# A planned attention and feed-forward kernel: other transfer costs in its planner, and an earlier second pair of heads

## The chip, the cores and the metric

The kernel runs on one core of one Trainium2 chip. The time is that of the device for one execution, in microseconds (us). The engines are TensorE (PE in the profile; PEld is its weight load), VectorE (DVE), ScalarE (ACT), GpSimd (POOL) and SyncE (SP), which issues every transfer here.

## The reference

```python
def _attn_ref(q, k, v, cap):                 # 4 batches, 12 heads, 448 positions, 64 columns
    scores = np.matmul(q, k.transpose(0, 1, 3, 2)) / np.sqrt(q.shape[-1])
    scores = cap * np.tanh(scores / cap)
    attn = np.exp(scores - np.max(scores, axis=-1, keepdims=True))
    return np.matmul(attn / (np.sum(attn, axis=-1, keepdims=True) + 1e-09), v)
def _moe_ref(x, w_in, w_out):                # 1792 x 768, 768 x 2048, 2048 x 768
    h = x @ w_in
    return (h * np.cos(h)) @ w_out
def _moe2_ref(x, w1, w2, w3, w_out):         # 768 x 1024 twice, 1024 x 1024, 1024 x 768
    return (((x @ w1) * (x @ w2)) @ w3) @ w_out
```

The output of the attention, with the heads side by side, goes through the first of the two feed-forward parts, and that through the second. The arrays of the attention are float32. The weights of the two feed-forward parts are float64.

## The kernel before

**Precision.** TensorE works on operands split into a high part (a rounded copy) and a low part (the rest). A product is then three matmuls, high by high, high by low and low by high: `mm3`, lines 389 to 391. The split is a copy (`copy`, line 363, executed at L365, L366 or L369) and a subtraction (`lo`, which goes through `tt`, L375). Weights arrive as words of 64 bits. `convert` makes float32 of them in four steps (L913 or L914, L919, L926, L930).

**Stages.** Three stages overlap in time. `columns` is the attention: the 48 heads are taken in 24 pairs, each with four chunks of 112 columns of keys, numbered g through all pairs. For a chunk, `c_S` makes the scores of two heads in a double bank of the PSUM (there are two), `c_exp` lets ScalarE take the tanh and then the exponential of them, and `c_PV` multiplies by V (L694) and sums the exponentials with a matmul by ones (L699). `c_sums` gathers the sums in four small transfers into `rs`, takes the reciprocal, writes it to `rs_d` and reads it back spread over the partitions into `rb`; `c_norm` multiplies by it on VectorE or GpSimd. `make_w34` multiplies the last two weights (w3 and w_out of the second feed-forward part) into one, in 16 runs, beside the attention. `moe1` and `moe2` are the two feed-forward parts.

**Two forms of the scores.** For the first `SLIM` pairs, `c_load` fetches q and k of a pair once (two heads on 128 partitions), `c_split` splits them, and `c_S` makes the scores with matmuls of 64 rows, two heads at once (L650). For the other pairs, `a_load` fetches each head twice, once for each half of the partitions, `a_split` puts high and low parts of k above each other, and the scores take matmuls of 128 rows (L660, L661). The tiles of q and k (`qr`, `kr`) have two planes of 448 columns and a ring of one slot. The slim form uses the first plane.

**The order of the work.** No order is written out by hand. Every operation is entered in a plan with a due time, the engines that can do it with a cost for each, what it reads and writes, and, for a transfer, its size `kb`. `schedule` simulates: at each moment it gives an idle engine the ready operation of the earliest due time, if its ring has a free slot. A due time is a rank and not a start: an operation may start before it. The order so found is fixed, and on the chip each engine takes its instructions in that order and waits for semaphores. A transfer costs 0.66 us on SyncE, then shares one line:

```python
if o.kb:
    line = max(line, end) + o.kb / self.RATE
    out = line + self.LATENCY
```

Readers of it become ready at `out` (and `HOP` later). Due times of the attention are `at(g)` = 10 + 3.03 g (lines 526 to 528); those of the first weight run lie 20 us ahead of its matmuls at 20, its loads another 14 us ahead, so -14 for the first w3 tile, and -9.1 and -6.5 for the first two w_out tiles. A load of q and k is due six chunks ahead of its pair, a split three, V two; only the first pair's q and k have -99.

**Edge.** `general` is a second program for large values of `cap` and does not run here.

Of the kernel before, what the change touches and what calls it, by code (L numbers as in the profile page):

```python
# [20 lines left out]
B, H, S, D = 4, 12, 448, 64  # L21
# [16 lines left out]
PAD = 64  # L38
# [98 lines left out]

class Plan:
    HOP = 0.25
    RATE, LATENCY = 250.0, 2.2  # L140
    SWITCH = 1.3


# [159 lines left out]
    ql=6, qs=3,  # L303
# [18 lines left out]
def tile_kernel(tc, *args):  # L322


    nc = tc.nc
    cap = args[3]
    program(tc, *args)
    with tc.tile_pool(name="large", bufs=1) as p:
        c = p.tile([1, 2], F32, name="cap2")
        large = p.tile([1, 1], mybir.dt.int32, name="large")  # L330
        nc.sync.dma_start(c[:, 0:1], cap.rearrange("(o n) -> o n", o=1))
        nc.vector.tensor_scalar(c[:, 1:2], c[:, 0:1], -1.0, None, op0=ALU.mult)
        nc.vector.tensor_tensor(c[:, 0:1], c[:, 0:1], c[:, 1:2], op=ALU.max)
        nc.vector.tensor_scalar(large, c[:, 0:1], CAP_MAX, None, op0=ALU.is_gt)
        with tc.If(nc.values_load(large[0:1, 0:1], min_val=0, max_val=1) > 0):
            program(tc, *args, general=True)
# [3 lines left out]
def program(  # L340
# [22 lines left out]
    def copy(due, dst, src, n, on, psum=False):  # L363
        opts = {
            "A": ("ACT", (0.051 if psum else 0.094) + n / 1200, lambda: ACT.copy(dst(), src())),  # L365
            "D": ("DVE", 0.068 + n / (960 if psum else 1920), lambda: DVE.tensor_copy(dst(), src()))  # L366
            + (() if psum else (True,)),
            "P": ("POOL", 0.16 + n / 1200,
                  lambda: POOL.tensor_scalar(dst(), src(), 1.0, 0.0, op0=ALU.mult, op1=ALU.add)),  # L369
        }  # L370
        plan.op(due, [opts[e] for e in on], r=[src], w=[dst])

    def tt(due, dst, a, b, n, op, on="D", psum=False):
        opts = {
            "D": ("DVE", 0.068 + n / 960, lambda: DVE.tensor_tensor(dst(), a(), b(), op=op))  # L375
            + (() if psum else (True,)),
            "P": ("POOL", 0.158 + n / 480, lambda: POOL.tensor_tensor(dst(), a(), b(), op=op)),
        }
        plan.op(due, [opts[e] for e in on], r=[a, b], w=[dst])

    def lo(due, dst, src, hi, n, on="PD", psum=False):
        tt(due, dst, src, hi.view(lambda t: t.bitcast(F32)), n, ALU.subtract, on, psum)

    def dma(due, dst, src, r=(), w=(), kb=115, write=False):
        plan.op(due, [("SP", 0.66, lambda: SP.dma_start(dst(), src()))], r=r, w=w,  # L385
                kb=kb)
# [17 lines left out]
    for name, kw in dict(const={}, xring={}, dram=dict(space=DRAM), psum=dict(space=PSUM), doubles=dict(space=PSUM), singles=dict(space=PSUM), attn={}, lp={},  # L404
                         wi=dict(side="right"), wp=dict(side="right"), yp=right, hp=right, mp=right, cv=right,
                         q2=right).items():
# [21 lines left out]
    class Scratch:  # L428
# [7 lines left out]
        def at(self, sub, pick=None):  # L436
            return Ref(self.item, sub, pick)
# [70 lines left out]
    A = {}  # L508
# [21 lines left out]
    qk, vt, st, sm, rs, rb, s_t, t_t, pt_t, ph_t, pv_t, zs_t, x32 = ({} for _ in range(13))  # L530

    def rows(j):
        return lambda t: t[j * D:(j + 1) * D]
# [4 lines left out]
    def a_load(i, g):  # L538
        b, h = divmod(i, H)
        qk[i] = A["qr"].new(), A["kr"].new()  # L540
        for it, src in zip(qk[i], (q2, k2)):
            for j in range(2):
                r = it.at(j, rows(j))
                dma(at(g) if i else -99.0, r, lambda src=src: src[b, h // 2].rearrange("(i d) s -> d i s", i=2),
                    w=[r], kb=230)
# [6 lines left out]
    def a_split(i, g):  # L552
        q, k = (Ref(x) for x in qk.pop(i))
        qh, ql, ks = (A[x].ref() for x in ("qh", "ql", "ks"))
        copy(at(g), ks, k, 2 * S, "PAD")
        low = Ref(ks.item, None, rows(1))
        lo(at(g), low, k.view(rows(1)), low, 2 * S)
        copy(at(g), qh, q, 2 * S, "PAD")
        lo(at(g), ql, q, qh, 2 * S)
        for j in range(2):  # L560
            st[i + j] = qh[:, j], ql[:, j], ks[:, j]
# [39 lines left out]


    NT = NC // 2
    SLIM = 3

    def c_load(i, g):
        if i // 2 >= SLIM:
            return a_load(i, g)
        b, h = divmod(i, H)
        qk[i] = A["qr"].new(), A["kr"].new()  # L610
        for it, src in zip(qk[i], (q2, k2)):
            r = it.at(0, lambda t: t[:, 0])
            dma(at(g) if i else -99.0, r, lambda src=src: src[b, h // 2], w=[r], kb=230)

    def c_split(i, g):
        if i // 2 >= SLIM:
            return a_split(i, g)
        q, k = (x.at(0, lambda t: t[:, 0]) for x in qk.pop(i))
        qh, ql, ks = (A[x].new() for x in ("qh", "ql", "ks"))
        kh, kl = (ks.at(j, lambda t, j=j: t[:, j]) for j in range(2))  # L620
        qh, ql = (x.at(0, lambda t: t[:, 0]) for x in (qh, ql))
        copy(at(g), kh, k, S, "PAD")
        lo(at(g), kl, k, kh, S)
        copy(at(g), qh, q, S, "PAD")
        lo(at(g), ql, q, qh, S)
        st[i] = (kh, qh), (kh, ql), (kl, qh)

    def c_consts():
# [4 lines left out]
    def cv_load(i, g):  # L633
        b, h = divmod(i, H)
        n, j = divmod(i, 2)
        if j == 0:
            vt[n] = A["v"].new()
        r = vt[n].at(j, lambda t: t[:, j])
        dma(at(g), r, lambda: v[b, h], w=[r])

    def c_S(n, k, g):
        s = s_t[n, k] = s_r.ref()
        if n < SLIM:
            terms = st[2 * n]
# [20 lines left out]
    def c_exp(n, k, g):  # L665
        s = s_t.pop((n, k))[:CP, :, :S]
        p = A["p"].ref()
        for j in range(2):
            if n < SLIM:
                ph_t[n, j, k] = p, j  # L670
# [37 lines left out]
    def c_sums(n, g):  # L708

        t, z = A["rs"].new(), zs_t.pop(n)  # L710
        for j in range(2):
            for k in range(2):
                q = Q * (2 * j + k)
                y = t.at((j, k), lambda x, j=j, k=k: x[j * D:(j + 1) * D, k])
                dma(at(g), y, z.view(lambda x, q=q: x[q:q + 1]), r=[z], w=[y], kb=100)
        r, d = Ref(t), rs_d.at(n, lambda d: d[n].rearrange("j (p c) -> (j p) c", p=D))
        s0, s1 = (r[:, k] for k in range(2))

        def f():
            DVE.tensor_tensor(s0(), s0(), s1(), op=ALU.add)  # L720
            DVE.reciprocal(s0(), s0())

        plan.op(at(g) + 3, [("DVE", 0.2, f)], r=[r], w=[r])
        dma(at(g) + 4, d, s0, r=[r], w=[d], kb=100, write=True)
        rb[n] = A["rb"].new()
        for k in range(2):
            y = rb[n].at(k, rows(k))
            dma(at(g) + 5, y, lambda k=k: rs_d.item.tile()[n, k].unsqueeze(0).to_broadcast([D, S]), r=[d], w=[y])
# [10 lines left out]
    def columns():  # L739
        one = c_consts()  # L740
        c_load(0, -2)
        c_split(0, -1)
        for g in range(-8, NT * NH + 16):
            of_pair(c_load, -G["ql"], g, NT)
            of_head(cv_load, -2, g, NT)
            of_pair(c_split, -G["qs"], g, NT)
            if 0 <= g < NT * NH:
                c_S(*divmod(g, NC), g)
                c_exp(*divmod(g, NC), g)
            of_two(lambda n, g: n < 2 and c_PV(n, [0], one, g), 3, g)  # L750
            of_two(lambda n, g: c_PV(n, [1] if n < 2 else [0, 1], one, g), 5, g)
            of_two(c_move, 6, g)
            of_two(c_sums, 6, g)
            of_two(lambda n, g: c_norm(n, at(g) + 11), 6, g)
            of_two(lambda n, g: a_out(2 * n + 1, at(g) + 14), 6, g)
        first = plan.move(s_r, hy_r, at(g), lambda k: ())
        plan.move(s_r, hy_r, at(g), lambda k: range(4), part_doubles, [first])
# [648 lines left out]
```

## Time and profile before

| | us |
|---|---|
| runs | 1070.08, 1067.01, 1069.99 (median 1069.99) |
| profiled execution, its own time | 1065.92 |
| its span, first to last instruction | 1064.1 |
| TensorE busy in it | 1045.1 (98%) |
| VectorE busy | 874.0 (82%) |
| ScalarE busy | 492.1 (46%) |
| GpSimd busy | 173.6 (16%) |

The profile is of one execution. Times in it count from its first instruction. A busy TensorE is one that has a matmul under way, and need not be at its peak rate. An idle engine costs time only where the engine that sets the end waits for it.

### The profile page before, as it was taken

To read this page: it belongs to the slowest core of one execution; us is meant where nothing else is said; L and a number is where in the kernel's file an instruction comes from. 1 tells how busy PE (TensorE), PEld (TensorE's weight loads), DVE (VectorE), ACT (ScalarE), POOL (GpSimd) and SP (SyncE) were. 2 spreads that over 40 slices of the span, in tenths; PEclk is the share of its full clock that TensorE was granted. 3 is DMA by queue.
4 is the path that set the end of the run, shared out by engine and by line. 5 is a ranking of instruction groups with operands and counts; after the bars stand their busy time and mean duration, and the time that the engine had idled before them with its cause. 6 is when DMAs were issued, how large, how long until landed. Compare 5 with 4: busy or idle time off the path is not lost.

```text
span 1064.1 us, 15654 instructions
## 1 busy us (share of the span) xinstructions
PE 1045.1 (98%) x5832; PEld 894.5 (84%) x5832; DVE 874.0 (82%) x1343; ACT 492.1 (46%) x649; POOL 173.6 (16%) x159
## 2 busy tenths in 40 slices
PE   6999998999999999999999999999999999999997
PEld 3677775777888888889999999999999999999997
DVE  7998667899999898788889878779899889667643
ACT  5877675886667665621253211122344245311121
POOL 4222110221342131210002100011313000000000
PEclk9999999999999999999999999999999999999999
DMA  7876976777667655428632422106555546221232
GB/s 232 220 215 179 245 213 188 213 202 243 203 194 235 207 159 156 154 77 277 208 104 81 144 60 59 46 15 204 189 182 193 156 136 217 98 88 60 61 93 104
DMA packets 82408, 167.86 MB, mean 158 GB/s; under 512 B 19602, under 2 KB 55698, under 8 KB 82322
## 3 DMA queue, kind: packets, MB, share of 16 engines
q1 hardware_dynamic: 82322, 166.76, 51.3%
q8 instruction: 48, 0.79, 0.3%
q14 instruction: 38, 0.31, 0.1%
HBM read 127.93 MB, written 38.62 MB: 157 GB/s over the span
## 4 chain that ended last, share of the span: by engine, by line
PE 93%; DVE 2%; issue 2%; DMA 1%; ACT 1%; SPq 0%; POOL 0%; DVEq 0%; ACTq 0%; POOLq 0%
PE bank L389 26%; PE bank L391 26%; PE bank L390 26%; PE bank L694 6%; PE double L660 3%; PE bank L699 3%; PE double L661 3%; DMA kr<-in_k 1%; DMA raw<-in_w3T 0%; DVE x L930 0%; SPq L385 0%; DVE x L926 0%; DVE ks L375 0%; DVE ql L375 0%; ACT double L675 0%
## 5 line engine op out<-in xcount | busy, mean ns | idle before, releaser
L389 PE MATMUL bank<-g,woh 128*128 128x448 f32 x384 | 140.3, 365 | 0.0
L389 PE MATMUL bank<-xh,wih 128*128 128x448 f32 x384 | 139.7, 364 | 0.0
L391 PE MATMUL bank<-xh,wil 128*128 128x448 f32 x384 | 139.2, 362 | 0.0
L391 PE MATMUL bank<-g,wol 128*128 128x448 f32 x384 | 139.0, 362 | 0.0
L390 PE MATMUL bank<-xl,wih 128*128 128x448 f32 x384 | 138.7, 361 | 0.0
L390 PE MATMUL bank<-g,woh 128*128 128x448 f32 x384 | 138.6, 361 | 0.0
L375 DVE TENSOR_TENSOR y<-bank,y 128x448 f32<-128x448 f32 x168 | 103.6, 618 | 41.5 <-PE bank L391 40.4
L365 ACT COPY hs<-bank 128x448 f32<-128x448 f32 x73 | 39.1, 535 | 180.8 <-PE bank L391 180.8
L675 ACT ACTIVATE double<-double,ts 112x896 f32<-112x896 f32 x96 | 93.8, 980 | 55.4 <-PE double L661 49.6
L675 ACT ACTIVATE p<-double,pac 112x896 f32<-112x896 f32 x96 | 96.3, 1012 | 1.8
L389 PEld LDWEIGHTS bank<-g,woh 128*128 128x128 f32 x384 | 72.1, 188 | 10.5 <-DVE wx L930 1.5
L694 PE MATMUL bank<-p,v 112*32 112x448 f32 x768 | 78.7, 549 | 0.0
L389 PEld LDWEIGHTS bank<-xh,wih 128*128 128x128 f32 x384 | 72.1, 188 | 7.7 <-issue 2.2
L391 PEld LDWEIGHTS bank<-g,wol 128*128 128x128 f32 x384 | 72.0, 188 | 5.4
L391 PEld LDWEIGHTS bank<-xh,wil 128*128 128x128 f32 x384 | 72.1, 188 | 5.2
L390 PEld LDWEIGHTS bank<-xl,wih 128*128 128x128 f32 x384 | 71.9, 187 | 4.9
L390 PEld LDWEIGHTS bank<-g,woh 128*128 128x128 f32 x384 | 71.9, 187 | 4.7
L389 PE MATMUL bank<-ab,w34h 128*128 128x448 f32 x192 | 69.7, 363 | 0.0
L391 PE MATMUL bank<-ab,w34l 128*128 128x448 f32 x192 | 69.5, 362 | 0.0
L390 PE MATMUL bank<-ab,w34h 128*128 128x448 f32 x192 | 69.3, 361 | 0.0
L660 PE MATMUL double<-qh,ks 128*112 128x448 f32 x168 | 61.5, 366 | 3.0 <-ACT p L675 3.0
L661 PE MATMUL double<-ql,ks 128*112 128x448 f32 x168 | 61.3, 365 | 0.0
(226 smaller groups left out, 2328.4 us busy)
## 6 DMA issues: line engine op xcount, KB each, us to landing
rawc<-in_w_out SPq DMA_DIRECT2D x16, 768.0 KB, 4.9
stq<-w_d SPq DMA_DIRECT2D x32, 384.0 KB, 3.3
qr<-in_q SPq DMA_DIRECT2D x45, 224.0 KB, 4.3
kr<-in_k SPq DMA_DIRECT2D x45, 224.0 KB, 4.8
rawc<-in_w_in SPq DMA_DIRECT2D x13, 768.0 KB, 5.4
raw<-in_w3T SPq DMA_DIRECT2D x16, 512.0 KB, 5.7
rawl<-in_w SPq DMA_DIRECT2D x10, 768.0 KB, 5.0
raw<-in_w_out SPq DMA_DIRECT2D x8, 768.0 KB, 6.5
```

Of the source, the lines that this page charges most:

```text
L365: "A": ("ACT", (0.051 if psum else 0.094) + n / 1200, lambda: ACT.copy(dst(), src())),
L375: "D": ("DVE", 0.068 + n / 960, lambda: DVE.tensor_tensor(dst(), a(), b(), op=op))
L389: PE.matmul(out, wh, xh, start=first, stop=False, skip_group_check=on)
L390: PE.matmul(out, wh, xl, start=False, stop=False, skip_group_check=on)
L391: PE.matmul(out, wl, xh, start=False, stop=last, skip_group_check=on)
L660: PE.matmul(o, w, qh(), start=True, stop=False)
L661: PE.matmul(o, w, ql(), start=False, stop=True)
L675: lambda f=f, x=x, o=o: ACT.activation(o(), s(), f, scale=x[:CP]))],
L694: PE.matmul(pv()[q * Q:(q + 1) * Q, :S], w()[:, j, c, d:d + Q], piece(j, c), **flags)
L699: PE.matmul(z()[q:q + Q, :S], one(), piece(j, 2 * c + k), start=c == 0, stop=c == NT - 1)
```

## The change

The planner's `RATE` and `LATENCY` get other values, and the five small transfers of a pair's sums count 10 KB where they counted 100 (the write and the four gathers; the two reads back keep their 115). `SLIM` goes from 3 to 4. In the slim form, the odd pair of two (pairs 1 and 3) takes the second plane of the tile of the pair ahead of it and no new tile. The first two pairs get early due times: loads -22 and -12, splits -15 and -13, and V of the two heads of the first pair -13.

```diff
--- before.py
+++ after.py
@@ -137,7 +137,7 @@
 
 class Plan:
     HOP = 0.25
-    RATE, LATENCY = 250.0, 2.2
+    RATE, LATENCY = 270.0, 1.3
     SWITCH = 1.3
 
 
@@ -601,28 +601,30 @@
 
 
     NT = NC // 2
-    SLIM = 3
+    SLIM = 4
 
     def c_load(i, g):
         if i // 2 >= SLIM:
             return a_load(i, g)
         b, h = divmod(i, H)
-        qk[i] = A["qr"].new(), A["kr"].new()
-        for it, src in zip(qk[i], (q2, k2)):
-            r = it.at(0, lambda t: t[:, 0])
-            dma(at(g) if i else -99.0, r, lambda src=src: src[b, h // 2], w=[r], kb=230)
+        m = i // 2 % 2
+        items = [x.item for x in qk[i - 2]] if m else [A[x].new() for x in ("qr", "kr")]
+        qk[i] = [it.at(m, lambda t: t[:, m]) for it in items]
+        for r, src in zip(qk[i], (q2, k2)):
+            dma(at(g) if i > 2 else 5 * i - 22.0, r, lambda src=src: src[b, h // 2], w=[r], kb=230)
 
     def c_split(i, g):
         if i // 2 >= SLIM:
             return a_split(i, g)
-        q, k = (x.at(0, lambda t: t[:, 0]) for x in qk.pop(i))
+        q, k = qk[i]
+        due = at(g) if i > 2 else i - 15.0
         qh, ql, ks = (A[x].new() for x in ("qh", "ql", "ks"))
         kh, kl = (ks.at(j, lambda t, j=j: t[:, j]) for j in range(2))
         qh, ql = (x.at(0, lambda t: t[:, 0]) for x in (qh, ql))
-        copy(at(g), kh, k, S, "PAD")
-        lo(at(g), kl, k, kh, S)
-        copy(at(g), qh, q, S, "PAD")
-        lo(at(g), ql, q, qh, S)
+        copy(due, kh, k, S, "PAD")
+        lo(due, kl, k, kh, S)
+        copy(due, qh, q, S, "PAD")
+        lo(due, ql, q, qh, S)
         st[i] = (kh, qh), (kh, ql), (kl, qh)
 
     def c_consts():
@@ -636,7 +638,7 @@
         if j == 0:
             vt[n] = A["v"].new()
         r = vt[n].at(j, lambda t: t[:, j])
-        dma(at(g), r, lambda: v[b, h], w=[r])
+        dma(at(g) if n else -13.0, r, lambda: v[b, h], w=[r])
 
     def c_S(n, k, g):
         s = s_t[n, k] = s_r.ref()
@@ -712,7 +714,7 @@
             for k in range(2):
                 q = Q * (2 * j + k)
                 y = t.at((j, k), lambda x, j=j, k=k: x[j * D:(j + 1) * D, k])
-                dma(at(g), y, z.view(lambda x, q=q: x[q:q + 1]), r=[z], w=[y], kb=100)
+                dma(at(g), y, z.view(lambda x, q=q: x[q:q + 1]), r=[z], w=[y], kb=10)
         r, d = Ref(t), rs_d.at(n, lambda d: d[n].rearrange("j (p c) -> (j p) c", p=D))
         s0, s1 = (r[:, k] for k in range(2))
 
@@ -721,7 +723,7 @@
             DVE.reciprocal(s0(), s0())
 
         plan.op(at(g) + 3, [("DVE", 0.2, f)], r=[r], w=[r])
-        dma(at(g) + 4, d, s0, r=[r], w=[d], kb=100, write=True)
+        dma(at(g) + 4, d, s0, r=[r], w=[d], kb=10, write=True)
         rb[n] = A["rb"].new()
         for k in range(2):
             y = rb[n].at(k, rows(k))
```

## Rows read from the trace of the kernel before

**Rows 1.** Windows: busy us (instructions) of PE, PEld, DVE, ACT, POOL; clock; DMA.

```profile
5.87:28.00 22.13, 17.90 (x120) 9.17 (x124) 19.79 (x21) 15.68 (x20) 11.27 (x11) 1.00 0.76 246
28.00:160.00 132.00, 131.83 (x913) 94.79 (x906) 107.27 (x165) 99.64 (x125) 30.03 (x30) 1.00 0.80 215
160.00:200.00 40.00, 37.04 (x261) 24.71 (x260) 32.17 (x52) 27.13 (x31) 6.35 (x6) 1.00 0.66 190
200.00:1058.00 858.00, 858.00 (x4546) 765.84 (x4544) 712.71 (x1098) 347.59 (x472) 125.60 (x108) 1.00 0.46 146
...
sum 1064.10, PE 1045.09 PEld 894.51 DVE 873.99 ACT 492.06 POOL 173.57; mean PE 174.18 PEld 149.09 DVE 145.66 ACT 82.01 POOL 28.93
```

**Rows 2.** Waits of PE: waiting line, releaser, us in total, times, longest.

```profile
PE double L650 <- DVE ks L366: 5.9, 1, 5.9
PE double L650 <- ACT p L675: 3.0, 2, 2.0
PE double L660 <- ACT p L675: 3.0, 1, 3.0
PE double L650 <- DVE ql L375: 1.2, 1, 1.2
```

**Rows 3.** Timeline of PE, 5 to 26 us: start, us, instruction, idle before.

```profile
12.96 2.86 PE L694 MATMUL bank<-p,v 112*32 112x448 f32 x16
...
21.64 0.46 PE L650 MATMUL double<-ql,ks 64*112 64x448 f32 x2 [1.17 <-DVE ql L375]
...
25.20 0.46 PE L650 MATMUL double<-qh,ks 64*112 64x448 f32 x2 [1.02 <-ACT p L675]
```

**Rows 4.** Timeline of POOL, DVE and ACT, 0 to 34 us.

```profile
7.20 0.65 POOL L914 TENSOR_SCALAR raw<-raw 128x512 f32<-128x512 f32 x1 [6.34 <-DMA raw<-in_w3T]
...
8.62 0.69 DVE L926 SCALAR_TENSOR_TENSOR x<-raw,x 128x512 uint32<-128x512 uint32 x1 [2.14 <-POOL x L919]
...
20.31 1.27 DVE L375 TENSOR_TENSOR ql<-qr,qh 128x448 fp32r<-128x448 f32 x1
...
9.40 1.90 ACT L675 ACTIVATE p<-double,pac 112x896 f32<-112x896 f32 x2
```

**Rows 5.** The tile qr, 0 to 8 us: its two loads, first and last start.

```profile
L385 SPq DMA_DIRECT2D qr<-in_q x2: 418/524/629, 1.2 to 5.8; - x2
...
DMA to landing us min/median/max: 3.2/5.7/8.2
```

**Rows 6.** Timeline of SP, POOL and ACT, 142 to 172 us.

```profile
156.10 0.54 SPq L385 DMA_DIRECT2D wi_d<-x  x1
...
160.59 1.72 POOL L919 TENSOR_SCALAR x<-raw 128x768 f32<-128x768 f32 x2 [11.41 <-DMA rs_d<-rs]
...
163.69 0.56 ACT L365 CAST xh<-x 128x448 fp32r<-128x448 f32 x1 [3.94 <-DVE x L375]
```

**Rows 7.** Timeline of PE, 36 to 48 us, around a slim and a full chunk.

```profile
42.32 0.34 PE L391 MATMUL bank<-w2h,w3l 128*128 128x384 f32 x1
...
43.38 0.44 PE L389 MATMUL bank<-w2h,w3h 128*128 128x384 f32 x1
...
45.87 0.34 PE L391 MATMUL bank<-w2h,w3l 128*128 128x384 f32 x1
...
46.85 0.34 PE L389 MATMUL bank<-w2h,w3h 128*128 128x384 f32 x1
```

**Rows 8.** Transfers, 28 to 200 us: count, KB, median us from issue to landing.

```profile
raw<-in_w3T SPq DMA_DIRECT2D x13, 512.0 KB, 5.9
...
rb<-rs_d SPq DMA_DIRECT2D x22, 112.0 KB, 3.4
...
rs<-zs SPq DMA_DIRECT2D x45, 1.8 KB, 3.4
rs_d<-rs SPq DMA_DIRECT2D x12, 3.5 KB, 4.0
```

**Rows 9.** The tile rb (0 to 480 us) and its reader (28 to 200 us).

```profile
  DMA rb<-rs_d: 2.7, 2
...
L375 DVE TENSOR_TENSOR x<-xs,rb x11: 612/618/828, 46.3 to 196.5; 128x448 f32<-128x448 f32 x11
```

## The prediction

> **What bounds the kernel now.** I read the windows first. Between 200 and 1058 us TensorE is busy all 858 of 858 us, and from 28 to 160 us it misses 0.17 us [rows 1]. So the kernel is TensorE work laid end to end, and the rest is the 19.0 us that the sum row leaves (1064.10 less 1045.09): 5.87 before the first matmul, 4.23 between 5.87 and 28, 2.96 between 160 and 200, 5.78 at the end and the 0.17. A new order of the same operations can gain only out of these; what it can lose has no such limit.
>
> The list of waits names them [rows 2]. The first 5.9 us wait for the split of K. Then come 2.0 and 1.0 us waiting for the exponential on ScalarE (3.0 in two waits), 1.2 us for `ql` from VectorE, and one wait of 3.0 us for an exponential much later. The timeline puts places to them: 1.17 us before 21.64 (second pair, the `ql` split late) and 1.02 us before 25.20 (second pair, its exponential late because its scores were) [rows 3]. The 2.0 us lie before the third chunk of the first pair: there are two double banks, and the first comes free when the exponential that runs from 9.40 has read it [rows 4].
>
> Why is `ql` of the second pair late? Its load stood late in SyncE's queue, issued about 5.8 us and landed 8.2 us later, behind the first two w_out tiles of 768 KB and the V of four heads [rows 5]; then its splits stood behind the weight conversions on VectorE, which after an idle of 2.14 us before 8.62 is busy 19.79 of 22.13 us [rows 1, 4]. The `ql` split ran from 20.31.
>
> The 3.0 us near 164 us are a queue effect. A spill of a weight tile was issued at 156.10, GpSimd's next conversion into that ring started at 160.59 after 11.41 us idle, VectorE's steps on it came after that, ScalarE's cast waited 3.94 us for VectorE, and the tanh behind that cast on ScalarE came too late for TensorE [rows 6]. Each engine takes its operations in the order that the planner wrote; one late transfer goes through four queues.
>
> **The change part by part.**
>
> *Second pair beside the first.* Today a new tile for q and k needs the ring's only slot, so the loads wait for the splits of the pair before. Now pairs 0 and 1 share one tile of two planes, and the due times put the loads behind q0, k0, the first w3 tile and V0, V1, ahead of both 768 KB tiles. When would they land? GpSimd began on the first w3 tile when it had landed; from there the queue moved the two w_out tiles, four V tiles and q1 (2208 KB) by 5.8 + 8.2 = 14.0 us. That is 6.8 us after GpSimd's start at 7.20 [rows 4], about 327 KB per us. V0, V1 and q1 (448 KB) then land at 8.6 us and k1 at 9.3 us: an estimate from those rows. The splits take the 2.14 us hole only in its last part and push the w3 conversion back by some 2 us, but take as much away from the stretch 15 to 22 us, where two of them ran 1.3 us each beside GpSimd. The scores of pair 1 can follow those of pair 0 as soon as a bank is free, near 15 us, and ScalarE continues without its hole. I therefore take the 1.17 and 1.02 us as gone. If the first weights, pushed back by 672 KB (2.1 us at that rate), leave TensorE without work instead, nothing is gained: bounds 0 and 2.2 us. I take the upper one, since TensorE then has both pair 1 and the weights to choose from, where it had one at a time. The 2.0 us stay: banks and exponentials of pair 0 are not touched. The 5.87 us stay too; its casts could go to another engine, a gain below 0.4 us that I leave out.
>
> *V sooner.* V lands several us earlier, but the first product with V starts at 12.96 directly behind the last scores [rows 3]. It waited for no V that shows: 0, and at most the 0.5 us of that hand-over.
>
> *A fourth slim pair.* Pair 3 now takes the form with 24 matmuls of 64 rows, two at once, in place of 16 of 128 rows. From the last matmul ahead of a chunk to the first behind it a slim chunk takes 43.38 - 42.32 = 1.06 us, a full one 46.85 - 45.87 = 0.98 us [rows 7]. Four chunks: +0.3 us of TensorE. It saves two of four loads of 224 KB, and its four splits have 448 columns and not 896. That cuts work on VectorE around 43 to 47 us, just ahead of the 0.17 us that TensorE lost between 28 and 160 us, so I count these as gone as well.
>
> *The planner's transfers.* A load of kb costs 0.66 + kb/250 + 2.2 us from issue in the plan, now 0.66 + kb/270 + 1.3; the small gathers count 10 KB in place of 100. Worked out, queueing apart, that is for `rs` 3.3 against 2.0, for `rs_d` 3.3 against 2.0, for `rb` (115) 3.3 against 2.4. The chip took 3.4, 4.0 and 3.4 us between 28 and 200 us, and 5.9 us for a w3 tile of 512 KB, where the plan has 4.9 and now 3.9 [rows 8]. So there the old figures are 0.1 to 1.0 us short and the new ones 1.0 to 2.0 us: operations that read a transfer get queued before it lands, and what stands behind them waits too. A transfer that is planned well ahead costs nothing by this, since its lead (12 to 14 us by the due times of the weights) covers it. From both sides: 0 if all have such leads; the upper end is in the slow rival below.
>
> The Trainium skill, page "DMA: Bandwidth & Descriptors", section "Anatomy of one DMA", gives a fixed part of about 2.0 us to a transfer, and its section "Latency and other measured facts" an HBM latency of 0.2 us on average and 2 us at high load, so it speaks against 1.3 us; the rows of this case agree, with 3.4 us for an `rs` gather of 1.8 KB [rows 8]. By it the slow rival would be the likely one.
>
> The whole plan is made anew from these figures, so the chain of 156 to 167 us will not come about in the same order. I take its 2.96 us as gone, but one transfer that is 1.5 us short (the middle of the shortfalls above) as reaching TensorE.
>
> *Sum:* -1.17 - 1.02 - 0.17 + 0.3 - 2.96 + 1.5 = -3.5 us. Against the profiled execution (1065.92 us, span 1064.1) that is 1062.4; the runs shown have a median of 1069.99, 4.1 us over it, so 1066.5 us is what I put down. 0.3% of it, 3.2 us, is about what a measurement can tell from no change.
>
> **The rivals.**
>
> *A stall as long as that at 164 us stays or comes elsewhere.* For it: the stretch 28 to 200 us holds attention, the weight product and the first loads of the next stage, and the old, more careful figures already gave one stall of 3 us. Against it: it was one in 172 us. Then -2.36 + 0.3 = -2.1, 1067.9 us, or 1069 with a stall of 4.
>
> *Slower: VectorE stands before transfers that the plan has too early.* The place is the chain `rs`, `rs_d`, `rb` of each pair, whose end is read by the multiplication on VectorE. Measured 3.4 + 4.0 + 3.4 = 10.8 us; old plan 9.8, 1.0 short; new plan 6.4, 4.4 short, that is 3.4 us worse for each pair. Between 28 and 160 us VectorE has 132.00 - 107.27 = 24.7 us idle, and pairs follow each other every 15.0 us ((196.5 - 46.3) / 10) [rows 1, 9], so 2.8 us of slack each. The whole shortfall of 4.4 us would overrun it by 1.6 us, 14 us over nine pairs; if only the 3.4 count, 0.6 us each and 5 us. For it: the landings. Against it: with 1.0 us short VectorE waited for `rb` only 2.7 us, in 2 of 24 pairs [rows 9]. It decides from about 3 us of wait per pair on. Time with 8 us lost to TensorE and the start won: 1070.0 - 2.1 + 8 = 1076.
>
> *The start doesn't gain.* VectorE is busy in 90% of 5.87 to 28 us [rows 1], so the early splits only push the weights, and the waits change their names: -0.17 + 0.3, 1070.1 us with the stall kept.
>
> **How the numbers follow.** The sum 0.40, a stall kept 0.33, VectorE before transfers 0.19, no gain at the start 0.08. Faster by over 0.3%: 0.33 out of the first and 0.08 out of the second: 0.41. Slower: 0.16 out of the third, 0.04 out of the second and 0.02 out of the fourth: 0.22. Within: 0.37. The range goes from all idle gained with no new wait (-2.36 + 0.3 - 2.96 = -5.0 and the scatter of the runs, 3 us between lowest and highest, on the lower side half: 1063.5, and 1 us more for the casts and the hand-over to V: 1062.0) to 1074, three quarters of the slow rival's loss.
>
> **What would show it.** Right: no wait of TensorE between 18 and 26 us, the second pair's splits before the w3 conversion, V landed before 9 us, 96 matmuls at the slim line in place of 72, no wait over 1.5 us between 28 and 200 us. Wrong: waits of VectorE for `rb`, `rs`, `kr` that add up to over 10 us before 200 us, a new wait of TensorE for the first `w3` or `w2` parts, or TensorE idle after 200 us, where it has none now.

## The result and the profile after

The changed kernel takes 1081.15 us (median of six runs, 1076.37 to 1084.01) against 1066.82 us for the kernel before in the same comparison (six runs): a ratio of 1.0123 [1.0095, 1.0150]. It is 1.2% slower. The two medians alone would give 1.0134. The forecast was 1066.5 us and a range of 1062 to 1074 us; the time lies above the range and on the other side of no change.

The profiled execution took 1084.01 us with a span of 1082.2. It is the slowest of the six, while that of before (1065.92) is shorter than all six runs of before, so the two profiles lie 18.1 us apart where the medians lie 14.3 apart. The windows of after (busy us and instructions of PE, PEld, DVE, ACT, POOL; granted clock; DMA), cut as in [rows 1], with the stretch up to 470 us apart:

```profile
5.87:28.00 22.13, 20.00 (x140) 9.50 (x144) 19.18 (x22) 17.64 (x22) 11.87 (x10) 1.00 0.79 270
28.00:160.00 132.00, 123.90 (x828) 88.08 (x818) 102.67 (x158) 91.60 (x118) 31.00 (x31) 0.97 0.71 197
160.00:200.00 40.00, 40.00 (x271) 27.18 (x271) 26.49 (x40) 28.09 (x35) 3.06 (x3) 0.96 0.66 196
200.00:470.00 270.00, 264.50 (x1566) 207.99 (x1565) 235.34 (x349) 187.78 (x215) 57.47 (x49) 0.99 0.62 187
...
sum 1082.20, PE 1053.98 PEld 896.33 DVE 868.48 ACT 501.51 POOL 173.42; mean PE 150.57 PEld 128.05 DVE 124.07 ACT 71.64 POOL 24.77
```

Two things stand in these rows. TensorE is idle for 8.10 us (132.00 less 123.90) between 28 and 160 us and for 5.50 us between 200 and 470 us, where it missed 0.17 and nothing before [rows 1]; between 160 and 200 us the 2.96 us of before are gone. Over the span its idle time is 1082.2 - 1053.98 = 28.2 us, 9.2 us more than before. And its busy time grew by 8.9 us for almost the same work (1053.98 against 1045.09): the granted clock reads 0.97, 0.96 and 0.99 where it read 1.00. Three stretches at half the clock lost 6.8 us of that (last section); what the other 2 us are these rows don't show. The mean over the span is 0.992, a deficit of 0.008 x 1082.2 = 8.7 us, but some 2 us of it lie behind the last matmul (0.69 over the last 6.6 us), where they cost nothing. 9.2 + 8.9 is the whole difference of the two spans, 18.1 us.

How often the clock falls differs between executions: over the six runs of after its mean is 0.992 to 0.998 (0.995 on average), over the 31 runs of before in the comparison of `start_2p3` 0.995 to 1.000 (0.997). So of what lies between the typical times some 2 us (0.002 x 1080) are the clock's, and the larger part is idle time.

The waits of PE between 28 and 470 us (waiting line, releaser, us in total, times, longest) are mostly for ScalarE, 11.0 of 13.6 us:

```profile
PE double L662 <- ACT p L677: 6.4, 4, 2.7
PE bank L389 <- ACT zs L365: 2.9, 1, 2.9
PE double L652 <- ACT p L677: 1.7, 2, 1.0
PE bank L389 <- DVE zs L366: 1.2, 1, 1.2
...
```

But ScalarE's own waits over the same stretch are for weights that have not landed:

```profile
ACT rawc L915 <- DMA rawc<-in_w_out: 14.8, 8, 4.1
ACT raw L915 <- DMA raw<-in_w3T: 11.7, 4, 3.4
ACT rawc L915 <- DMA rawc<-in_w_in: 8.8, 7, 2.1
...
ACT raw L915 <- DMA raw<-in_w_out: 2.6, 2, 1.3
```

That is 37.9 us in 21 waits; the same rows of before add up to 10.9 us in 8. VectorE's waits for the sums' chain are the second group, 30.2 us in 19 waits where before had 2.7 in 2 [rows 9]:

```profile
DVE x L375 <- DMA rb<-rs_d: 18.6, 11, 5.9
DVE rs L722 <- DMA rs<-zs: 11.6, 8, 5.1
```

One stall shows the path. From the timelines of SP, ACT and PE between 102 and 114 us (SPq is SyncE issuing a transfer):

```profile
102.04 1.69 SPq L385 DMA_DIRECT2D raw<-in_w3T  x2
```

```profile
109.16 0.68 ACT L915 ACTIVATE raw<-raw 128x512 f32<-128x512 f32 x1 [3.07 <-DMA raw<-in_w3T]
109.72 1.88 ACT L677 ACTIVATE double<-double,ts 112x896 f32<-112x896 f32 x2
111.50 1.92 ACT L677 ACTIVATE p<-double,pac 112x896 f32<-112x896 f32 x2
```

```profile
107.38 0.37 PE L663 MATMUL double<-ql,ks 128*112 128x448 f32 x1
...
109.49 0.34 PE L391 MATMUL bank<-w2h,w3l 128*128 128x384 f32 x1
112.57 0.71 PE L662 MATMUL double<-qh,ks 128*112 128x448 f32 x1 [2.75 <-ACT p L677]
113.09 0.57 PE L663 MATMUL double<-ql,ks 128*112 128x448 f32 x1
```

The scores were done by 107.75. Their tanh stood on ScalarE behind the first conversion step of a w3 tile whose load was issued at 102.04 and landed 7.0 us later; by the plan's figures (0.66 + 512/270 + 1.3) it takes 3.9. ScalarE waited 3.07 us, then TensorE 2.75 us for an exponential that waited for no transfer itself. The matmul behind it takes 0.57 us where the same one took 0.37 before the stall. The two other long waits of TensorE, 2.56 us up to 159.31 and 2.86 us up to 255.53, have the same step (L915) on ScalarE ahead of what they wait for:

```profile
156.45 0.90 ACT L915 ACTIVATE raw<-raw 128x768 f32<-128x768 f32 x1 [3.43 <-DVE qh L366]
```

```profile
253.27 0.91 ACT L915 ACTIVATE rawc<-rawc 128x768 f32<-128x768 f32 x1 [1.48 <-DMA rawc<-in_w_in]
```

By the profile the first of these two waited for VectorE's copy of q and not for a landing, so not every stall is a late weight alone.

The second of the two w3 loads issued from 102.04 shows why it had no lead. On the chain that ended last, in order of time:

```profile
102.25 1.08 DVE x L932
...
103.39 7.06 DMA raw<-in_w3T
```

L932 is the last conversion step of an earlier tile. The load of the next one goes out 0.06 us after that step has freed its slot. The due time may lie 14 us ahead of the first use; the slot does not. Between 28 and 200 us SyncE waited nine times for L932, 14.5 us together, before it could issue a load. This was not new: in before it waited for the same step (L930 there) seven times, 11.2 us.

The transfers themselves are hardly slower than before [rows 8]: `rb` takes 0.5 us and `rs` 0.2 us more, w3 0.4 us and `rs_d` 0.8 us less. Over 28 to 200 us (count, KB, median us from issue to landing)

```profile
raw<-in_w3T SPq DMA_DIRECT2D x13, 512.0 KB, 5.5
...
rb<-rs_d SPq DMA_DIRECT2D x22, 112.0 KB, 3.9
...
rs<-zs SPq DMA_DIRECT2D x44, 1.8 KB, 3.6
rs_d<-rs SPq DMA_DIRECT2D x11, 3.5 KB, 3.2
```

The start, on the other hand, came nearly as forecast. The second pair's splits (two timeline rows of VectorE) run behind the first of VectorE's two steps on the first w3 tile (8.27) and ahead of all its other work on weights, and the pair's scores (two rows of PE, with the first matmul on weights) start at 16.98 us, against 20.01 in the trace of before:

```profile
9.19 0.39 DVE L366 CAST ks<-kr 128x448 fp32r<-128x448 f32 x1
...
10.02 0.62 DVE L375 TENSOR_TENSOR ks<-kr,ks 128x448 fp32r<-128x448 f32 x1
```

```profile
16.98 0.46 PE L652 MATMUL double<-qh,ks 64*112 64x448 f32 x2
...
21.57 0.44 PE L389 MATMUL bank<-w2h,w3h 128*128 128x384 f32 x1
```

TensorE is idle 2.13 us between 5.87 and 28 us instead of 4.23.

### The profile page after: what moved, and what is told of

It is laid out like the page before. It is cut to its first block, busy times and chain, and to the rows that moved or that the text cites. A ratio compares the mean times of both kernels' runs of the same rounds, so it can differ in the third digit from the quotient of the medians.

```text
span 1082.2 us, 15710 instructions
## 1 busy us (share of the span) xinstructions
PE 1054.0 (97%) x5840; PEld 896.3 (83%) x5840; DVE 868.5 (80%) x1332; ACT 501.5 (46%) x660; POOL 173.4 (16%) x159
## 4 chain that ended last, share of the span: by engine, by line
PE 78%; DMA 7%; DVE 7%; ACT 3%; issue 3%; SPq 1%; POOL 0%; DVEq 0%; ACTq 0%; POOLq 0%
PE bank L389 23%; PE bank L390 23%; PE bank L391 23%; PE bank L696 4%; DMA raw<-in_w3T 2%; PE bank L701 2%; DMA rb<-rs_d 2%; DMA rs<-zs 1%; PE double L662 1%; PE double L663 1%; SPq L385 1%; ACT p L677 1%; ACT double L677 1%; PE double L652 1%; DMA rawc<-in_w_out 1%
## 5 line engine op out<-in xcount | busy, mean ns | idle before, releaser
L696 PE MATMUL bank<-p,v 112*32 112x448 f32 x768 | 81.6, 566 | 0.0
L696 PEld LDWEIGHTS bank<-p,v 112*32 112x32 f32 x768 | 22.9, 113 | 45.6 <-issue 42.2
```

The lines of the kernel that those rows point to most:

```text
L696: PE.matmul(pv()[q * Q:(q + 1) * Q, :S], w()[:, j, c, d:d + Q], piece(j, c), **flags)
```

## The experiments

The question was which part loses the time and by which path. Explanation one: the plan's short transfers, through waits of VectorE for the sums' chain, through waits of ScalarE for weights, or both. Rival two: the early second pair and the fourth slim pair. Rival three: any new order loses, since the old one was lucky. Theories A, B and C in the expectations are VectorE's waits of explanation one, rival two and rival three, D is ScalarE's waits, E both.

All times together; "idle" is TensorE's between 28 and 470 us, "clock" the mean granted clock of the one profiled execution, its end behind the last matmul included, "sums" the waits of VectorE's readers of `rb` and `rs` for them and "weights" ScalarE's waits for weight loads, both from 28 to 470 us. Ratios are to the kernel before in the same comparison (median 1066.82 us for after, 1068.6 to 1069.2 us for the others).

| kernel | us | ratio [95%] | idle | clock | sums | weights |
|---|---|---|---|---|---|---|
| before | | 1 | 3.1 | 1.000 | 2.7 | 10.9 |
| after | 1081.15 | 1.0123 [1.0095, 1.0150] | 13.6 | 0.992 | 30.2 | 37.9 |
| start_only | 1072.98 | 1.0043 [1.0029, 1.0057] | 7.5 | 0.995 | 3.1 | 7.2 |
| model_only | 1085.36 | 1.0159 [1.0120, 1.0198] | 11.8 | 0.992 | 31.4 | 36.0 |
| latency_back | 1071.20 | 1.0020 [1.0002, 1.0039] | 8.0 | 0.999 | 8.7 | 24.0 |
| kb_back | 1069.04 | 1.0001 [0.9987, 1.0015] | 6.1 | 0.998 | 17.2 | 34.2 |
| latency_3 | 1068.74 | 0.9997 [0.9982, 1.0011] | 6.1 | 0.999 | 0 | 7.0 |
| plan_2p1 | 1067.42 | 0.9982 [0.9971, 0.9994] | 2.1 | 0.999 | 1.2 | 9.5 |
| plan_2p3 | 1067.05 | 0.9981 [0.9968, 0.9994] | 3.0 | 0.999 | 0.5 | 9.6 |
| chain_lat | 1080.30 | 1.0091 [1.0066, 1.0116] | 14.2 | 0.994 | 3.3 | 35.7 |
| weights_lat | 1077.84 | 1.0070 [1.0043, 1.0097] | 10.9 | 0.995 | 37.5 | 16.4 |
| qkv_lat | 1078.45 | 1.0078 [1.0053, 1.0103] | 12.2 | 0.997 | 36.1 | 40.9 |
| chain_weights_lat | 1065.95 | 0.9969 [0.9957, 0.9981] | 2.8 | 0.999 | 3.1 | 9.0 |
| all_lat | 1066.02 | 0.9973 [0.9961, 0.9985] | 4.2 | 0.998 | 4.5 | 9.3 |
| cw_near | 1069.11 | 0.9995 [0.9978, 1.0013] | 4.4 | 0.997 | 2.7 | 11.7 |
| cw_no_start | 1067.90 | 0.9994 [0.9976, 1.0012] | 5.0 | 0.999 | 5.3 | 15.4 |
| start_slim3 | 1072.98 | 1.0038 [1.0022, 1.0054] | 9.2 | 0.994 | 2.2 | 9.1 |
| start_2p3 | 1068.64 | 1.0003 [0.9993, 1.0012] | 5.2 | 0.998 | 3.9 | 6.5 |
| chain_pool | 1076.30 | 1.0081 [1.0053, 1.0109] | 9.4 | 0.996 | 8.7 | 0 |
| pool_only | 1081.15 | 1.0136 [1.0101, 1.0172] | 14.0 | 0.997 | 33.1 | 0 |

**The two halves of the change.** Each of the two kernels undoes one half: `start_only` has the old figures, `model_only` the old start.

```diff
 # start_only, from after
-    RATE, LATENCY = 270.0, 1.3
+    RATE, LATENCY = 250.0, 2.2
-                dma(at(g), y, z.view(lambda x, q=q: x[q:q + 1]), r=[z], w=[y], kb=10)
+                dma(at(g), y, z.view(lambda x, q=q: x[q:q + 1]), r=[z], w=[y], kb=100)
-        dma(at(g) + 4, d, s0, r=[r], w=[d], kb=10, write=True)
+        dma(at(g) + 4, d, s0, r=[r], w=[d], kb=100, write=True)
 # model_only, from before: the same lines, the other way
```

> The changed kernel with the planner's old transfer costs (250, 2.2, small transfers at 100 KB); the earlier second pair, the earlier V and the fourth slim pair stay. Theory A (the shorter transfer costs queue readers before their data, VectorE stands, TensorE runs dry): the loss goes, TensorE waits under 4 us in all between 28 and 470 us, VectorE waits for rb and rs under 5 us, time 1062 to 1067. Theory B (the new start and the fourth slim pair disturb the rest of the order): the loss stays, 1078 to 1084. Theory C (any new order of so tight a plan costs about as much): 1072 or more, with other waits.

> The kernel before with the new transfer costs alone (270, 1.3, small transfers at 10 KB). Theory A: 1078 to 1088, VectorE waits over 20 us for rb and rs between 28 and 470 us, and stretches at a granted clock of half appear after TensorE's longer waits. Theory B: 1066 to 1070, as before. Theory C: 1072 or more.

The figures alone lose more than the whole change: 1.0159. The waits of VectorE between 28 and 470 us in `model_only` have the pattern of after, and the granted clock is as low:

```profile
DVE x L375 <- DMA rb<-rs_d: 21.1, 10, 5.5
DVE rs L720 <- DMA rs<-zs: 10.3, 10, 4.1
```

`start_only` has few of these waits (3.1 and 7.2 us, as before) and still loses 0.4%; its 1072.98 us is in the range of rival three, so that one had to be tried. Its timelines show the stall of [rows 6] again, by the same queues: GpSimd behind a spill, ScalarE behind VectorE's conversion, the tanh at 165.99 behind that.

```profile
160.47 0.88 POOL L921 TENSOR_SCALAR x<-raw 128x768 f32<-128x768 f32 x1 [11.50 <-DMA wi_d<-x]
```

```profile
165.24 0.84 ACT L365 CAST wih<-x 128x768 fp32r<-128x768 f32 x1 [4.18 <-DVE x L932]
165.99 0.97 ACT L677 ACTIVATE double<-double,ts 112x896 f32<-112x896 f32 x1
```

**Which figure.** Two kernels put one of them back, from after.

```diff
 # latency_back
-    RATE, LATENCY = 270.0, 1.3
+    RATE, LATENCY = 270.0, 2.2
 # kb_back: kb=100 in the five small transfers
```

> The changed kernel with 2.2 us of latency again, rate 270 and small transfers at 10 KB kept. Theory A, with the latency as its main term (0.9 us on every transfer, three in a row for each pair): 1064 to 1071, VectorE's waits for rb and rs under 10 us. If the small transfers' size is the main term (0.4 us each): 1076 or more. Theory B: 1078 or more.

> The changed kernel with the small transfers at 100 KB again, rate 270 and latency 1.3 kept. Theory A with the latency as main term: part of the loss stays, 1073 to 1082. If the size of the small transfers is the main term: 1064 to 1071. Theory B: 1078 or more.

Either one takes back most of the loss (1.0020 and 1.0001), so neither figure is the main term by itself. In `kb_back` the waits of VectorE fall from 30.2 to 17.2 us, but those of ScalarE stay at 34.2 us, and its figures (2.3 us for `rs` and `rs_d`, 2.4 for `rb`, 3.9 for w3) are still 1.0 to 2.0 us short of the landings in [rows 8]; so neither sum of waits prices the loss by itself.

**Is it any new order?** Two controls are the kernel before with the latency a little moved, which changes the order and leaves the figures fit; the third is after with a latency that brings the plan to the measured landings (0.66 + 10/270 + 3.0 = 3.7 us for `rs` and `rs_d`, 4.1 for `rb`, 5.6 for w3).

```diff
 # plan_2p1, plan_2p3, from before
-    RATE, LATENCY = 250.0, 2.2
+    RATE, LATENCY = 250.0, 2.1      # or 2.3
 # latency_3, from after
-    RATE, LATENCY = 270.0, 1.3
+    RATE, LATENCY = 270.0, 3.0
```

> The kernel before with its latency at 2.1 in place of 2.2 us: an order made anew, with transfers planned as well as before. Theory A: 1066 to 1071, waits for rb and rs under 8 us. Theory C (an order that was not tried and picked costs by itself): 1072 to 1084, with waits of TensorE of other causes.

> The kernel before with its latency at 2.3 in place of 2.2 us. Theory A: 1065 to 1070, waits for rb and rs under 5 us. Theory C: 1072 to 1084.

> The changed kernel with 3.0 us of latency, rate 270 and small transfers at 10 KB kept: its plan for the three small transfers is 3.7, 3.7 and 4.1 us, at or over most landings. Theory A: waits for rb and rs under 5 us and 1064 to 1070, at or under the kernel with 2.2. Theory C: no trend with the latency, up to 1080.

Both controls are 0.2% faster than before: a new order does not lose as such, and the old one was not lucky. `latency_3` comes out level (0.9997), with everything else of the change in it. At 270 KB per us and 10 KB, the latencies 1.3, 2.2 and 3.0 give 1081, 1071 and 1069 us.

**Which transfers.** A transfer now gets a latency of its own in the plan; nothing else is touched. With it the sums' chain alone, the weight loads alone, the loads of q, k and V alone, and the first two together are planned near what they measured.

```diff
-                    out = line + self.LATENCY
+                    out = line + (o.lat or self.LATENCY)
 # chain_lat: rs, rs_d, rb
+                dma(at(g), y, z.view(lambda x, q=q: x[q:q + 1]), r=[z], w=[y], kb=10, lat=2.7)
+        dma(at(g) + 4, d, s0, r=[r], w=[d], kb=10, write=True, lat=3.3)
+            dma(at(g) + 5, y, lambda k=k: rs_d.item.tile()[n, k].unsqueeze(0).to_broadcast([D, S]), r=[d], w=[y], lat=2.3)
 # weights_lat, in convert()
+        dma(due - 14, r, lambda: src, w=[r], kb=n, lat=3.0)
 # qkv_lat: lat=3.0 in the loads of q, k and V
 # chain_weights_lat: chain_lat and weights_lat
```

> The changed kernel with the measured landings given to the three transfers of each pair's sums alone (planned at 3.4, 4.0 and 3.4 us); every other transfer keeps rate 270 and latency 1.3. Theory A, the chain of the sums as its place: VectorE's waits for rb and rs fall from 30 us under 8, time 1066 to 1072, near the kernel with all latencies at 2.2. If the early loads of q, k and weights cost as much as the chain: 1074 to 1080. Theory C (the new order as such): no relation, 1068 to 1084.

> The changed kernel with 3.0 us of latency for the loads of 64-bit weights alone (planned at 5.6 us for a w3 tile, 6.5 for a w_out tile), all other transfers at rate 270 and latency 1.3. Theory D (ScalarE takes a weight conversion before its load has landed and the tanh behind it comes late; waits of 38 us in the changed kernel against 11 before): ScalarE's waits for weight loads under 15 us, time 1068 to 1074. Theory A (VectorE before rb and rs): 1078 or more.

> The changed kernel with 3.0 us of latency for the loads of q, k and V alone. Neither theory A nor D has its place here: 1076 to 1084. If late q and k (VectorE hardly waits for them by the profile) were the cause: 1072 or less.

> The changed kernel with measured landings for the sums' three transfers and 3.0 us of latency for the loads of 64-bit weights. Theory E (both queues count, either alone is enough to stall): 1064 to 1070, VectorE's and ScalarE's waits for transfers as before the change. Theory D alone: as with the weights alone.

In `chain_lat` the wait that the slow rival of the prediction named is nearly gone, and the loss is not (1.0091). Waits between 28 and 470 us, of VectorE and of ScalarE:

```profile
DVE rs L723 <- DMA rs<-zs: 2.4, 3, 1.4
DVE x L375 <- DMA rb<-rs_d: 0.9, 2, 0.7
```

```profile
ACT rawc L916 <- DMA rawc<-in_w_out: 14.3, 7, 5.0
ACT raw L916 <- DMA raw<-in_w3T: 9.2, 6, 2.9
ACT rawc L916 <- DMA rawc<-in_w_in: 8.5, 4, 4.2
```

`weights_lat` is the mirror of it: ScalarE's waits fall to 16.4 us, VectorE's stay (37.5), and more than half of the loss stays (1.0070).

```profile
DVE x L375 <- DMA rb<-rs_d: 27.9, 12, 5.6
DVE rs L723 <- DMA rs<-zs: 9.6, 11, 2.2
```

`qkv_lat`, which mends neither, keeps both and 1.0078. Of these four, only the one with both mended has lost the idle time and the loss: 0.9969. The windows of `chain_weights_lat`:

```profile
28.00:160.00 132.00, 130.45 (x909) 94.38 (x906) 110.84 (x161) 101.00 (x132) 38.73 (x36) 1.00 0.77 214
160.00:200.00 40.00, 40.00 (x276) 27.59 (x275) 31.88 (x52) 28.43 (x31) 7.18 (x5) 1.00 0.69 194
200.00:470.00 270.00, 268.75 (x1599) 213.21 (x1598) 243.67 (x359) 178.71 (x203) 67.09 (x57) 1.00 0.61 184
```

TensorE misses 1.55, 0 and 1.25 us, the clock is back at 1.00, and 909 matmuls stand between 28 and 160 us, nearly the 913 of [rows 1].

**Neighbours of that, and the start.** A single plan can be lucky, so four more kernels stand around these: `all_lat` (all three groups), `cw_near` (chain and weights, each latency 0.1 longer), `cw_no_start` (the same planned latencies as `chain_weights_lat`, with the start of before), and `start_2p3` (`start_only` with 2.3). `start_slim3` takes the fourth slim pair out of `start_only`.

```diff
 # cw_near, from chain_weights_lat: lat 2.7, 3.3, 2.3, 3.0 become 2.8, 3.4, 2.4, 3.1
 # start_2p3, from start_only
-    RATE, LATENCY = 250.0, 2.2
+    RATE, LATENCY = 250.0, 2.3
 # start_slim3, from start_only
-    SLIM = 4
+    SLIM = 3
```

> The changed kernel with measured landings for the sums' transfers, 3.0 us of latency for the loads of 64-bit weights and for those of q, k and V. Theory E (the more of the loads that attention and weights wait for are planned as they land, the fewer stalls): 1063 to 1067, waits for transfers of VectorE and ScalarE under 15 us together. If the one good run was luck: 1070 or more.

> The kernel with measured landings for the sums and the weights, each 0.1 us longer: another order of the same care. Theory E: 1064 to 1068. If the one good run was luck: 1070 to 1080.

> The kernel before (three slim pairs, late second pair) with rate 270, latency 1.3, small transfers at 10 KB, and measured landings for the sums and the weights. Theory E with the start worth its 2.2 us: 1066 to 1070. If the start is worth nothing: 1064 to 1067. If the careful landings only help together with the early start: 1072 or more.

> The changed kernel with the old transfer costs and 2.3 us of latency. If the 4 us that the early start lost under the old costs lay in the one order found (the late spill near 160 us again): 1064 to 1069. If the early loads themselves disturb what follows: 1071 to 1076.

> The early second pair and the early V with the old transfer costs and three slim pairs. If the fourth slim pair costs what the start wins (the run with both was 0.4% slower than before): 1064 to 1067, faster than before by the 2 us of the start. If the early loads disturb what follows: 1071 to 1075.

The neighbours agree: 0.9973, 0.9995 and 0.9994, each far from 1.0123, though `cw_near` came 1 us over its expected range. Among them the order alone moves the time by 0.3%: `chain_weights_lat` and `cw_near` differ by 3 us and by nothing but 0.1 us in four figures. So the start is worth at most some 2 us (0.9969 with it, 0.9994 without, and the intervals touch), and these runs can't tell it from the scatter of orders: in the trace of `chain_weights_lat` itself TensorE is idle for 3.38 us between 5.87 and 28 us, which is 0.85 us less than before and not 2.1. The same goes for the loss of `start_only`: 0.1 us more latency takes it from 1.0043 to 1.0003, so the start and the slim pair do not force it, and without the fourth slim pair it is 1.0038. The stall near 165 us shown above is not what makes the difference: between 160 and 200 us TensorE is idle for 2.47 us in `start_only`, 2.67 in `start_2p3`, 4.85 in `start_slim3` and 2.96 in before. What `start_only` has over `start_2p3` is 2.72 us of idle time between 200 and 470 us against 0.22, and a lower clock, 0.995 against 0.998.

**Past ScalarE's queue.** If weights reach TensorE only because tanh and exponential stand behind the first conversion step on ScalarE, that step can be moved to GpSimd. `chain_pool` does this on top of `chain_lat`, `pool_only` on after.

```diff
-        ][early:], r=[r], w=[r])
+        ][1:], r=[r], w=[r])
```

> The kernel with measured landings for the sums' transfers alone (1080), and ScalarE no longer allowed the first step of a weight conversion: all of them go to GpSimd, whose queue TensorE needs less. No landing of a weight is planned longer. Theory E with ScalarE's queue as the way in which late weights reach TensorE: 1065 to 1071. If the weights themselves come too late for TensorE, by whichever queue: 1076 or more.

> The changed kernel with all first steps of weight conversions on GpSimd, no landing planned longer. VectorE still stands before rb and rs (30 us). Theory E: part of the loss, 1072 to 1079. If ScalarE's queue were the whole of it: 1065 to 1070.

`pool_only` is as slow as after (1.0136) and over its expected range; the sums' chain in it still waits 33.1 us. `chain_pool` missed what I hoped of ScalarE's queue: ScalarE waits for no weight at all, and the time is 1.0081, at the edge of the other branch, where weights come late by whichever queue. Its windows and two timeline rows:

```profile
28.00:160.00 132.00, 128.49 (x881) 92.98 (x874) 107.52 (x158) 88.82 (x111) 46.58 (x45) 0.99 0.75 201
160.00:200.00 40.00, 35.56 (x229) 24.66 (x231) 29.20 (x41) 25.25 (x29) 8.66 (x7) 0.96 0.66 192
```

```profile
164.10 1.71 POOL L922 TENSOR_SCALAR x<-raw 128x768 f32<-128x768 f32 x2 [10.13 <-DMA wi_d<-x]
```

```profile
168.25 0.83 ACT L365 CAST wih<-x 128x768 fp32r<-128x768 f32 x1 [5.57 <-DVE x L933]
```

Between 28 and 160 us it did help: TensorE misses 3.51 us there instead of 9.15 in `chain_lat`. Then the stall behind the spill took 4.44 us, and the clock reads 0.96 there. GpSimd now had more to do ahead of that spill; whether this made the stall or the order did was not tried.

**What sets the time in all of them.** Take the span of before, 1064.1 us; subtract 2.1 where the start is new; add the idle between 28 and 470 us beyond 3.1, and the lost clock, (1 - clock) times the span. For `kb_back` that is 1064.1 - 2.1 + 2.9 + 2.1 = 1067.1, measured 1067.6; for after 1081.1, measured 1082.2; for `chain_weights_lat` 1062.7, measured 1063.0. Over the 20 profiled executions 17 agree within 1.2 us, the other three (`model_only`, `qkv_lat`, `pool_only`) are 2.8 to 3.1 us longer than it gives. The sum is rough in two terms: the start's own gain is 2.1 us in after but 0.85 in `chain_weights_lat`, and the lost clock includes some 2 us behind the last matmul in after. With that said, TensorE's idle time and its clock account for the time; the sums of waits on VectorE and ScalarE say where to look, not what it costs.

## Why the prediction was wrong

**The step that failed** is the one on the planner's transfers, in two sentences: "A transfer that is planned well ahead costs nothing by this, since its lead (12 to 14 us by the due times of the weights) covers it", and the term that followed, +1.5 us for one short transfer reaching TensorE. The lead is a due time and the ring's slot decides: a w3 load was issued when the last conversion step freed its tile, and its first reader stood in ScalarE's queue by a figure of 3.9 us, with tanh and exponential behind it. The slots gave no lead in before either (11.2 us of SyncE's waits against 14.5), but there the figure of 4.9 us was nearer to the 5.9 us of the landing. Not one wait of 1.5 us came of it but ten, up to 2.86 us long: 13.6 us of idle between 28 and 470 us where the sum had 0.17 + 2.96 - 0.17 - 2.96 + 1.5 = 1.5. The step was mis-sized by 12 us. The prediction's own signs of being wrong came true: up to 200 us VectorE's readers of `rb`, `rs` and `kr` waited 16.7 us for them, and TensorE was idle behind 200 us.

**A term that was missing.** The sum had no price for the granted clock. The 2.96 us of idle in [rows 6]'s stretch had cost nothing more; the windows there read 1.00 [rows 1]. In the profiled execution of after 6.8 us were lost to the clock on top of the idle time; over the runs it is some 2 us more than in before (0.995 against 0.997). The base of the forecast was high as well: 1069.99 us from three runs, 1066.82 from six. The lower end of the range was added up 0.5 us too low (1063.5 less 1 is 1062.5), which decides nothing.

**The slow rival** had the mechanism, operations queued ahead of a transfer's landing, and half of the place. Its waits came: 30.2 us for `rb` and `rs` up to 470 us. Its time, 1076, came nearer than the forecast. But it held the chain of the sums for the only path, and `chain_lat` refutes that: with 3.3 us of such waits the kernel still loses 0.9%. Mending one path alone left 0.7 to 0.9% (`chain_lat`, `weights_lat`), mending both nothing (`chain_weights_lat`). That both have to be closed is not shown: `kb_back` has 17.2 and 34.2 us of these waits and loses nothing. Its argument against itself, that a plan 1.0 us short had cost only 2.7 us of waits, held only for that shortfall.

**The page that I weighed.** The Trainium skill, page "DMA: Bandwidth & Descriptors", section "Anatomy of one DMA", gives about 2.0 us of fixed cost, fitted to transfers that GpSimd issues; here SyncE issues them all. I set these 2.0 us against the plan's 1.3, but the plan charges 0.66 us on SyncE besides, so its fixed part is 1.96 us. The Trainium skill's figure did not speak against the new costs, and the slow rival does not follow from it. The runs go above that figure: the 1.8 KB gathers landed in 3.6 us, and fixed parts of 1.96, 2.86 and 3.66 us in the plan gave 1081, 1071 and 1069 us (after, `latency_back`, `latency_3`). What spoke for the slow rival were the landings of [rows 8], and I gave it 0.19 all the same.

**What held.** The start: 2.1 us of idle time gained in the trace where 2.2 were forecast, the second pair's splits ahead of the weights but for one step, no wait between 18 and 26 us, 96 matmuls at the slim line, the 2.00 us before the third chunk unchanged, and V of no effect. The 2.96 us near 164 us left that place in after, as I had taken it, but 2.56 us stand just ahead of it, up to 159.31 us, and the likes of it came back in `start_only`, `start_2p3`, `start_slim3` and `chain_pool`. That it starts from a spill was inferred, as the row of GpSimd in [rows 6] names `rs_d`; the same row of `start_only` names the spill. The 0.17 us that I counted as gone did not go: waits of 0.95, 0.70 and 0.76 us end at 35.05, 50.26 and 62.90 us.

**What stays open.** Why `kb_back` loses so little idle time with 34.2 us of ScalarE's waits in it, the only one of the eight plans that keep such short figures for the sums, the weights or both that is not at least 0.7% slower; by which queue short weight loads reach TensorE when the first step is not on ScalarE (`chain_pool`); whether the start gains its 2 us in the time; and what the fourth slim pair costs, which no run separates from the scatter of orders.

## What to carry to other kernels

A planner's figure for a transfer should be the measured time from issue to landing under load, for each kind of transfer: figures between 0.3 us short and 0.7 us long of it lost nothing here (`latency_3`), figures 1.0 to 2.0 us short lost 1.2% in after and 1.6% in `model_only`, though in `kb_back`, where `rs` and `rs_d` alone are planned 0.3 us longer, nothing was lost. A due time far ahead is no lead if a ring's slot decides when the load is issued; look at what releases the issuing queue. And before an order made anew by a planner is judged, move one of its figures by 0.1 us as a control: here that alone moved the time by 0.2 to 0.4%.

## What the runs showed of the hardware

The granted clock fell to half, the lower of its two levels (1.2 GHz), at short stalls. Windows of after, the first two equally long, the others at two more stalls:

```profile
112.08:118.91 6.83, 6.34 (x27) 3.03 (x31) 1.67 (x3) 3.89 (x5) 0.67 (x1) 0.50 0.97 258
118.91:125.74 6.83, 6.83 (x54) 4.60 (x47) 3.29 (x7) 3.56 (x5) 0.95 (x1) 1.00 0.31 87
159.87:163.28 3.41, 3.41 (x18) 1.77 (x20) 3.03 (x4) 3.15 (x4) 0.00 (x0) 0.50 0.83 199
255.44:258.86 3.42, 3.33 (x9) 2.98 (x10) 3.04 (x6) 1.44 (x4) 0.44 (x1) 0.50 0.62 205
```

At 0.50 TensorE got through 27 matmuls, at 1.00 through 54. The three stretches began within 0.6 us of the end of idle times of 2.75, 2.56 and 2.86 us and hold 13.66 us, so 6.8 us of full-speed work were lost in them, as much as the idle times themselves (8.2 us) to within a fifth. The 2.96 us of idle in before came with no such stretch, nor did waits of 2.33 and 2.55 us in `latency_back`, whose clock reads 1.00 from 28 to 470 us. What decides it these runs don't show.

Landing times scatter widely under load: 512 KB of w3 took a median of 5.5 to 5.9 us and 7.0 us in the stall above, where 0.66 + 512/270 + 1.3 is 3.9.
